# Prologue and first block of an attention and MoE kernel: ACT, VectorE and POOL in the order the code names them, with the weight conversion spread over the rounds

## The chip, the cores and the metric

The kernel runs on one core of one Trainium2 chip. The metric is the device time in microseconds (us) of one execution; 1224.36 us is the median of three runs of the kernel before. The engines are TensorE (PE in the rows; PEld is its weight load), VectorE (DVE), ScalarE (ACT), GpSimd (POOL) and SyncE (SP), which issues most of the DMAs.

## The reference

Chunked attention, then a dense gated layer, then a top-1 mixture of experts with a skip condition, over 4608 tokens of 512 features:

```python
scores = q_c @ k_c^T / sqrt(64)            # 8 batches, 8 heads, chunks of 64 of 576
attn   = softmax(scores);  x = attn @ v_c  # x: 4608 x 512
h = x @ w_in                               # 512 x 2048, w_in in float64
g = h * sigmoid(1.702 * h)
x = (g @ w_out)                            # 2048 x 512, w_out in float64
out = x
for tokens with x @ w_skip > 0:            # 8 experts, 512 x 1024 x 512
    e = argmax(x @ w_gate)
    out += softmax(x @ w_gate)[e] * relu(x @ w1[e]) @ w2[e]
```

All of it is to hold to float32. The kernel therefore splits each operand of a large product into a high part (`hi`, a type that TensorE takes at full rate) and a rest (`lo`), and adds three products: hi·hi, hi·lo, lo·hi.

## The kernel before

**Blocks and rounds.** The 4608 tokens are nine blocks of 512 (`j`), each of four tiles of 128. The dense layer runs block by block, and in a block over 16 rounds (`i`), one for each 128 of the 2048 hidden features. A round has `emit_h` (line 289: 12 matmuls h(i), with the weights `whi[i]`, `wlo[i]` and the activations `xh`, `xl`; then tanh on ScalarE and `sg` on VectorE), `emit_g` (line 303: `gh` on ScalarE, `gl` on VectorE) and `emit_y` (line 310: 12 matmuls y(i) into the four banks `ys`). h has two PSUM banks, so h(i+2) can start when sg(i) has been computed. After the nine blocks come the experts; they are not touched.

**Attention.** A tile's attention (`Att`, line 109) has `a` (transposes of q and k into qT, kT, copies on ScalarE), `b` (scores, maxima and differences on VectorE, exp on ScalarE), `c0` (sum, reciprocal and scaling on VectorE), `c1` (transposes pT, copy on ScalarE) and `d` (products with v, two copies into x1 on ScalarE). The four tiles of block 0 go through it in the prologue, in the seven turns of the loop over `tau` (line 710). The tiles of the next block go through it in the rounds of the block before: `burst` (line 214) has the scores of one tile and the v products of the tile before it, in the rounds 1, 4, 7, 10 and 13 of block 0 (`BURSTS`); `c0` and `c1` follow two rounds later, `a` stands one round ahead. Scores, v products, and the transposes of the rounds share two banks (`at`). At a block's end `split_x1` (line 280) makes `xh` and `xl` of the next block.

**The conversion of the weights.** w_in and w_out arrive as float64 in 32 halves of 128 x 512 (`Half`, line 232; half 2i is w_in of round i, half 2i+1 is w_out). No engine reads float64, so the bits are taken apart: `s0` makes `r` (from the high word) and `lf` (from the low word) on ScalarE; `s1` shifts `r` (line 262) and merges the sign (line 263) on VectorE and adds `lf` on POOL (line 264); `s3` makes `hi` on ScalarE (line 276) and `lo` on VectorE (line 277). Three buffers hold the raw halves; `load` issues one DMA of 512 KB on SP. `tick` (line 694) is one step m of this: s1 of half m, s0 of half m+1, s3 of half m-1, and the load of half m+3. `lf` has one buffer. 33 steps do all.

**What sets the order.** The program is recorded in the order of the code, and a planner then places the instructions of each engine by its own estimate of when their inputs are ready. Each engine executes its list in order and waits at each instruction for its inputs. The code calls `tick` once in each of the turns 1 to 6 and twice in each round of block 0, until the 33 steps are done.

Of the kernel before, what the change touches and what calls it, by code (L numbers as in the profile page):

```python
# [9 lines left out]
F32 = mybir.dt.float32  # L10
# [11 lines left out]
def kernel(  # L22
# [14 lines left out]
    PE, ACT, DVE, POOL, SP = nc.tensor, nc.scalar, nc.vector, nc.gpsimd, nc.sync  # L37
# [5 lines left out]
    P = 128  # L43
# [3 lines left out]
    NF = DFF // P  # L47
    BT = 512
    TPB = BT // P
# [11 lines left out]

    BURSTS = {0: (1, 4, 7, 10, 13)}
    BURSTN = (1, 5, 9, 13)
    NXT = NT // SL + NE + NSING + 2
    BIG = float(1 << 20)

# [4 lines left out]
    mp = ctx.enter_context(tc.tile_pool(name="main", bufs=1))  # L71
# [7 lines left out]
    def bank(shape, tag, name):  # L79
# [10 lines left out]
        fill=0.0, base=0, channel_multiplier=-1,  # L90
# [13 lines left out]
    emeta = cp.tile([1, 2, NE], U32, name="emeta")  # L104
    meta = cp.tile([1, 3, NXT], U32, name="meta")
    wgT = cp.tile([P, KD, NE + 1], F32, name="wgT")
# [123 lines left out]
    HW = KD * P  # L230

    class Half:
# [14 lines left out]
        def s0(self):  # L247
            bits = self.raw.bitcast(U32).rearrange("p (n two) -> p n two", two=2)
            self.hw = bits[:, :, 1]
            hwf = self.raw.bitcast(F32).rearrange("p (n two) -> p n two", two=2)[:, :, 1]  # L250
            self.r = mp.tile([P, HW], F32, tag="x2", name="r", bufs=4)
            self.lf = mp.tile([P, HW], F32, tag="junk", name="lf")


            ACT.activation(out=self.r, in_=hwf, func=AF.Abs, scale=2.0 ** -112)
            ACT.activation(out=self.lf.bitcast(U32), in_=bits[:, :, 0], func=AF.Copy, scale=2.0 ** -29)

        def s1(self):
# [3 lines left out]
            DVE.tensor_scalar(ru, ru, 3, None, op0=ALU.logical_shift_left)  # L262
            DVE.scalar_tensor_tensor(au, self.hw, 0x80000000, ru, op0=ALU.bitwise_and, op1=ALU.bitwise_or)
            POOL.tensor_tensor(au, au, self.lf.bitcast(U32), op=ALU.add)

        def s2(self):
            pass

        def s3(self):
            i, h = self.i, self.half  # L270
# [9 lines left out]
    def split_x1(x1):  # L280
        xh = mp.tile([P, KD, BT], F32R, tag="xh", name="xh")
        xl = mp.tile([P, KD, BT], F32R, tag="xl", name="xl")
        for kk in range(KD):
            src = x1[kk // 2][:, kk % 2]
            ACT.copy(out=xh[:, kk], in_=src)
            DVE.tensor_tensor(xl[:, kk], src, xh[:, kk].bitcast(F32), op=ALU.subtract)
        return xh, xl
# [12 lines left out]
        DVE.scalar_tensor_tensor(sg, sg, 1.0, ps, op0=ALU.add, op1=ALU.mult)  # L300
        return sg

    def emit_g(sg):
        gh = mp.tile([P, BT], F32R, tag="gh", name="gh", bufs=2)
        gl = mp.tile([P, BT], F32R, tag="gl", name="gl", bufs=2)
        ACT.activation(out=gh, in_=sg, func=AF.Copy, scale=0.5)  # L306
        DVE.scalar_tensor_tensor(gl, sg, 0.5, gh.bitcast(F32), op0=ALU.mult, op1=ALU.subtract)  # L307
        return gh, gl

# [127 lines left out]
    def extras():  # L437
# [7 lines left out]
        def wide(nm):  # L445
            t = m2.tile([P, DM], F32, tag="o", name=nm, bufs=2)
            return t[0:1, 0:NXT * NB2].rearrange("o (x b) -> o x b", b=NB2)

        xb = [1, NXT, NB2]
        rem, tu = m2s([1, NE], "rem"), m2s([1, NE], "tu", U32)  # L450
        bc, b0, b1 = m2s([1, 1, NB2], "bc"), m2s([1, 1, NB2], "b0"), m2s([1, 1, NB2], "b1")
        row0, dp = m2s([1, 1, NB2], "row0"), m2s([1, 1], "dp")
        ix, bj, cx = m2s([1, NXT, 1], "ix"), m2s([1, NXT, 1], "bj"), m2s([1, NXT, 1], "cx")

# [190 lines left out]
    fp = fstack.enter_context(tc.tile_pool(name="f64", bufs=1))  # L645
# [25 lines left out]
    x1 = new_x1()  # L671
    A = [Att(t, x1, t * P, ("y", "at", "h", "h"), pro_buf(t), ios[t]) for t in range(TPB)]
    halves = [Half(m) for m in range(2 * NF)]
# [18 lines left out]
    tick_n = [0]  # L692

    def tick():
        m = tick_n[0]
        tick_n[0] += 1
        if m == 0:
            halves[0].s0()
        if m < 2 * NF:
            halves[m].s1()  # L700
        if 1 <= m <= 2 * NF:
            halves[m - 1].s2()
        if m + 1 < 2 * NF:
            halves[m + 1].s0()
        if 1 <= m <= 2 * NF:
            halves[m - 1].s3()
        if m + 3 < 2 * NF:
            halves[m + 3].load()

    for tau in range(TPB + 3):  # L710
        if 0 <= tau - 2 < TPB:
            A[tau - 2].c0()
        if tau < TPB:
            A[tau].a()
        if 0 <= tau - 1 < TPB:
            A[tau - 1].b()
        if 0 <= tau - 2 < TPB:
            A[tau - 2].c1()
        if 0 <= tau - 3 < TPB:
            A[tau - 3].d()  # L720
        if tau >= 1:
            tick()
    for g in range(2):
        SP.dma_start(out=tv[g], in_=z)
    xh, xl = split_x1(x1)

    fill, late = [], []
    NST = NT // P - TPB
# [2 lines left out]
    for j in range(NB - 1):  # L731
        for i in BURSTS.get(j, BURSTN):
            round_of[j * NF + i] = len(round_of)
# [4 lines left out]
    for j in range(NB):  # L738
        lastb = j + 1 == NB
        if not lastb:  # L740
            x1 = new_x1()
        else:
            rs.close()
            rawp = rs.enter_context(tc.tile_pool(name="raw", bufs=2, side="right", reuse_waits="tile"))
            for _ in range(4):
                load_next()
        ys = [bank([P, DM], "y", "yps") for _ in range(TPB)]
        prev = None
        nf = len(fill)
        for i in range(NF):  # L750
            R = j * NF + i
            nc_ = round_of.get(R - 2)
            if nc_ is not None and nc_ < NST:
                St[nc_].c0()
            sg = emit_h(i, xh, xl)
            span = NF // 2 - 2 if lastb else NF - 5
            nfill = -(-len(fill) // (span - i)) if i < span else 0
            if nfill:
                fill.pop(0)()
                nfill -= 1  # L760
            if j == 0:
                tick()
                if i == 7:
                    gate_load()
                elif i == 11:
                    gate_rows()
            g = emit_g(sg)
            if prev is not None:
                emit_y(i - 1, prev, ys)
            na = round_of.get(R + 1)  # L770
            if na is not None and na < NST:
                St[na].a()
                if na + 1 < NST:
                    St[na + 1].load_qk()
            if nc_ is not None and nc_ < NST:
                St[nc_].c1()
            kb = round_of.get(R)
            if kb is not None:
                if kb:
                    St[kb - 1].x1 = x1  # L780
                burst(St[kb] if kb < NST else None, St[kb - 1] if kb else None)
                if kb < NST:
                    St[kb].load_v()
            if j == 0:
                tick()
            for _ in range(nfill):
                fill.pop(0)()
            if late and (i >= span or late[0][0] < j):
                late.pop(0)[1]()
            if lastb:  # L790
                if prev is not None:
                    conv_next2()
                if i == NF // 2:
                    gstack.close()
                    m2 = ctx.enter_context(tc.tile_pool(name="m2", bufs=1, reuse_waits="tile"))
                    for s in range(NEARLY):
                        slots[s].list(first_row(s))
                if i >= NF // 2 + 2 and i - NF // 2 - 2 < NEARLY:
                    slots[i - NF // 2 - 2].gather((NB - 1) * BT)
            prev = g  # L800
        if j == 0:
            while tick_n[0] <= 2 * NF:
                tick()
            fstack.close()
            gstack = ExitStack()
            gp = gstack.enter_context(tc.tile_pool(name="gates", bufs=1, reuse_waits="tile"))
            wg = gp.tile([P, NE, DM], F32, name="wg")
            ws = gp.tile([P, DM], F32, name="ws")
            SP.dma_start(out=ws, in_=w_skip.rearrange("(o d) -> o d", o=1).to_broadcast([P, DM]))
            SP.dma_start(  # L810
                out=wg, in_=wgd[0:NE].rearrange("(o e) d -> o e d", o=1).to_broadcast([P, NE, DM]))
        if not lastb:
            xhn = split_x1(x1)
            emit_y(NF - 1, prev, ys)
            xh, xl = xhn
        else:
            slots[0].trans()
            emit_y(NF - 1, prev, ys)
            conv_next2()
        xs = evac_y(j, ys)  # L820
        lg = new_lg()
        if not lastb:
            fill = [lambda t=t, e=e, lg=lg, xs=xs: dot(lg, xs, t, e) for t in range(TPB) for e in range(NE + 1)]
            rt = route(j, lg)
            if j == NB - 3:
                rt.insert(3, order)
            late += [(j + 1, f) for f in rt]


    jx = m2.tile([1, NXT, 1], F32, name="jx")  # L830
    jw = m2.tile([1, NXT, 1], F32, name="jw")
    jm = m2.tile([1, NXT, 1], F32, name="jm")
# [103 lines left out]
```

## Time and profile before

| | us |
|---|---|
| median of three runs (1224.11, 1226.07, 1224.36) | 1224.36 |
| the profiled execution's own time | 1227.84 |
| its span, first to last instruction | 1226.1 |
| TensorE busy in the span | 1182.7 (96%) |
| VectorE busy | 783.9 (64%) |
| ScalarE busy | 490.2 (40%) |
| POOL busy | 144.6 (12%) |

How to read it: a busy time is the sum of an engine's instructions, an average over stages. A timeline row gives start, duration, engine, line, operation and tiles of one or several like instructions, and in brackets the idle time of the engine just before and what ended it. Matmuls overlap in the pipeline, so their rows are longer than their distance from one to the next.

### The profile page before, as it was taken

The numbers are of one execution on the slowest core, as the hardware profiler recorded it, in microseconds if no ns is written. First come the engines' busy times: TensorE is split into PE (matmuls) and PEld (weight loads), VectorE is DVE, ScalarE is ACT, GpSimd is POOL, SyncE is SP. The second block draws the span as 40 slices with busy tenths as digits, with TensorE's granted clock in tenths as the row PEclk, the third lists the DMA queues.
The fourth block names the chain that finished last, engine by engine and source line by source line (L and its number), as shares of the span: only waits on it lengthen the run. The fifth ranks groups of instructions, "written<-read, shape, count | busy, mean of one in ns | idle before, by whom it ended". The sixth has DMA issues, their size and how long they took to land. (4 is left out here: it accounts for less than half of the span.)

```text
span 1226.1 us, 20893 instructions
## 1 busy us (share of the span) xinstructions
PE 1182.7 (96%) x7984; PEld 991.8 (81%) x7984; DVE 783.9 (64%) x1771; ACT 490.2 (40%) x825; POOL 144.6 (12%) x137
## 2 busy tenths in 40 slices
PE   6798999999999999999999999999999999999995
PEld 4576788888888888888888888888788989999885
DVE  5889578369349548647736935943985686665531
ACT  5867443343332333324334333332344454444320
POOL 2344000010010010000001001001021023231110
PEclk9999999999999999999999999999999999999998
DMA  9756331131122113113113113202344677666540
GB/s 211 208 175 178 112 102 27 44 104 26 27 68 78 28 31 107 32 31 95 35 36 104 26 28 92 55 10 69 130 139 131 215 170 265 215 228 227 195 144 8
DMA packets 181848, 129.00 MB, mean 105 GB/s; under 512 B 122336, under 2 KB 155360, under 8 KB 181617
## 3 DMA queue, kind: packets, MB, share of 16 engines
q1 hardware_dynamic: 177072, 117.09, 33.4%
q0 software_dynamic: 4672, 10.54, 2.5%
q8 instruction: 64, 1.05, 0.4%
q14 instruction: 40, 0.32, 0.1%
HBM read 103.59 MB, written 25.04 MB: 105 GB/s over the span
## 5 line engine op out<-in xcount | busy, mean ns | idle before, releaser
L316 PE MATMUL yps<-whi,gh 128*128 128x512 f32 x576 | 228.7, 397 | 6.4 <-ACT gh L306 6.4
L296 PE MATMUL hps<-xh,whi 128*128 128x512 f32 x576 | 231.6, 405 | 3.2 <-DVE sg L300 3.2
L296 PE MATMUL hps<-xl,whi 128*128 128x512 f32 x576 | 227.5, 395 | 0.0
L296 PE MATMUL hps<-xh,wlo 128*128 128x512 f32 x576 | 227.0, 394 | 0.0
L317 PE MATMUL yps<-wlo,gh 128*128 128x512 f32 x576 | 225.6, 392 | 0.0
L300 DVE SCALAR_TENSOR_TENSOR sg<-sg,hps 128x512 f32<-128x512 f32 x144 | 98.3, 684 | 172.1 <-ACT sg L299 171.1
L353 DVE CUSTOM_DVE_ANT_0 junk<-x,wg 128x512 f32<-128x512 f32 x256 | 175.8, 687 | 4.0
L543 DVE TENSOR_TENSOR elo<-rawe,ehi 128x1024 fp32r<-128x1024 f32 x88 | 107.6, 1224 | 84.6 <-ACT ehi L542 84.5
L320 PE MATMUL yps<-whi,gl 128*128 128x512 f32 x576 | 156.0, 393 | 0.0
L299 ACT ACTIVATE sg<-hps 128x512 f32<-128x512 f32 x144 | 85.8, 598 | 163.4 <-PE hps L296 163.2
L542 ACT CAST ehi<-rawe 128x1024 fp32r<-128x1024 f32 x88 | 92.3, 1049 | 139.6 <-PE h2p L608 69.4
L306 ACT ACTIVATE gh<-sg 128x512 fp32r<-128x512 f32 x144 | 91.0, 632 | 118.3 <-DVE sg L300 104.8
L316 PEld LDWEIGHTS yps<-whi,gh 128*128 128x128 f32 x576 | 108.3, 188 | 30.9 <-ACT gh L306 7.8
L296 PEld LDWEIGHTS hps<-xh,whi 128*128 128x128 f32 x576 | 108.5, 190 | 26.3 <-DVE sg L300 4.1
L296 PEld LDWEIGHTS hps<-xh,wlo 128*128 128x128 f32 x576 | 108.9, 189 | 22.6
L320 PEld LDWEIGHTS yps<-whi,gl 128*128 128x128 f32 x576 | 108.0, 189 | 22.6 <-DVE gl L307 0.3
L317 PEld LDWEIGHTS yps<-wlo,gh 128*128 128x128 f32 x576 | 108.5, 188 | 21.8
L296 PEld LDWEIGHTS hps<-xl,whi 128*128 128x128 f32 x576 | 109.2, 190 | 20.6
L307 DVE SCALAR_TENSOR_TENSOR gl<-sg,gh 128x512 fp32r<-128x512 f32 x144 | 99.0, 688 | 33.4 <-ACT gh L306 21.7
L406 POOL DMA_INDIRECT tab<-pr,pos x36 | 37.8, 1049 | 682.3 <-DVE st L166 335.0
L608 PE MATMUL h2p<-xT,ehi 128*128 128x256 f32 x640 | 117.2, 283 | 0.0
L608 PEld LDWEIGHTS h2p<-xT,ehi 128*128 128x128 f32 x640 | 101.9, 191 | 2.6
(172 smaller groups left out, 1520.5 us busy)
## 6 DMA issues: line engine op xcount, KB each, us to landing
rawe<-in_moe_w_dram SPq DMA_DIRECT2D x88, 512.0 KB, 4.0
v<-in_v_dram SPq DMA_DIRECT2D x144, 64.0 KB, 2.7
x2d<-x SPq DMA_DIRECT2D x36, 256.0 KB, 3.1
out_dram<-x SPq DMA_DIRECT2D x36, 256.0 KB, 3.8
q<-in_q_dram SPq DMA_DIRECT2D x32, 256.0 KB, 3.7
k<-in_k_dram SPq DMA_DIRECT2D x32, 256.0 KB, 3.7
raw<-in_moe_w_in_dram SPq DMA_DIRECT2D x16, 512.0 KB, 4.0
raw<-in_moe_w_out_dram SPq DMA_DIRECT2D x16, 512.0 KB, 3.3
```

The source lines that it names most:

```text
L296: PE.matmul(ps, a, b[:, kk], start=(n == 0), stop=(n == 3 * KD - 1))
L299: ACT.activation(out=sg, in_=ps, func=AF.Tanh, scale=0.851)
L300: DVE.scalar_tensor_tensor(sg, sg, 1.0, ps, op0=ALU.add, op1=ALU.mult)
L306: ACT.activation(out=gh, in_=sg, func=AF.Copy, scale=0.5)
L307: DVE.scalar_tensor_tensor(gl, sg, 0.5, gh.bitcast(F32), op0=ALU.mult, op1=ALU.subtract)
L316: PE.matmul(ys[t], gh[:, cs], wh, start=first, stop=False)
L317: PE.matmul(ys[t], gh[:, cs], wl, start=False, stop=False)
L320: PE.matmul(ys[t], gl[:, cs], wh, start=False, stop=last)
L353: DVE.tensor_tensor_reduce(junk, xs[t], wg[:, e, :] if e < NE else ws, 1.0, 0.0, ALU.mult, ALU.add, lg[:, t, e:e + 1])
L542: ACT.copy(out=hi, in_=raw)
L543: DVE.tensor_tensor(lo, raw, hi.bitcast(F32), op=ALU.subtract)
L608: PE.matmul(ps[:, f], a[:, c], self.xT[:, b, kk], start=(m == 0), stop=(m == 3 * KD - 1))
```

## The change

It hands the planner three engines' lists as they are written: from the loop over `tau` to the end of block 0, `tc.manual_schedule` makes ScalarE, VectorE and POOL take their instructions in the order of the code. TensorE and SP are still placed by the planner. The code's order is changed with it: two steps more in the turns 5 and 6 make eight by the end of the prologue (`NTICK0`); the other 25 are spread evenly up to round 14 (`ticks_by`: 10 steps done after round 0, then 12, 13, 15, 17, 18, ... 33), in each round the first of them in two halves: `tick1` (s1) between gh and gl, `tick2` (s3, s0, load) behind gl; a second one stands before the burst. `split_x1` of block 0 moves ahead of the last two steps of the prologue. In a step s3 now stands ahead of s0. `lf` gets a second buffer. The empty `s2` goes.

```diff
+    NTICK0 = 8
...
-            self.lf = mp.tile([P, HW], F32, tag="junk", name="lf")
+            pool, tag = ((mp, "junk"), (fp, "lf"))[self.half]
+            self.lf = pool.tile([P, HW], F32, tag=tag, name="lf")
...
-    def emit_g(sg):
+    def emit_g(sg, between=None):
...
         ACT.activation(out=gh, in_=sg, func=AF.Copy, scale=0.5)
+        if between is not None:
+            between()
         DVE.scalar_tensor_tensor(gl, sg, 0.5, gh.bitcast(F32), op0=ALU.mult, op1=ALU.subtract)
...
+    def tick1():
         m = tick_n[0]
-        tick_n[0] += 1
         if m == 0:
             halves[0].s0()
         if m < 2 * NF:
             halves[m].s1()
+
+    def tick2():
+        m = tick_n[0]
+        tick_n[0] += 1
         if 1 <= m <= 2 * NF:
-            halves[m - 1].s2()
+            halves[m - 1].s3()
         if m + 1 < 2 * NF:
             halves[m + 1].s0()
-        if 1 <= m <= 2 * NF:
-            halves[m - 1].s3()
         if m + 3 < 2 * NF:
             halves[m + 3].load()
 
+    def ticks_by(i):
+
+        return min(2 * NF + 1, NTICK0 - (-(2 * NF + 1 - NTICK0) * (i + 1) // (NF - 1)))
+
+    inorder = ExitStack()
+    inorder.enter_context(tc.manual_schedule(engines={ACT.engine, DVE.engine, POOL.engine}))
     for tau in range(TPB + 3):
...
+        if tau == TPB + 2:
+            xh, xl = split_x1(x1)
         if tau >= 1:
+            tick()
+        if tau > TPB:
             tick()
...
+            mid = None
             if j == 0:
-                tick()
...
+                if tick_n[0] < ticks_by(i):
+                    mid = tick1
+            g = emit_g(sg, mid)
+            if mid is not None:
+                tick2()
...
+            while j == 0 and tick_n[0] < ticks_by(i):
+                tick()
...
-            if j == 0:
-                tick()
...
         if j == 0:
-            while tick_n[0] <= 2 * NF:
-                tick()
+            inorder.close()
```

Three places of the lists show what moves. A number behind a name is the tile's; the changed file has its lines up to 23 later.

ScalarE at the end of the prologue, before: `r`, `lf` and `hi` are the conversion, line 212 is a copy into x1, line 285 is xh.

```order
L189 COPY bA_97<-pTp_418 128x512
L255 ACTIVATE r_480<-raw64_412 128x512
L212 COPY x1_99<-pv0_424 128x2x128
L256 ACTIVATE lf_481<-raw64_412 128x512
L276 CAST whi_484<-a_476 128x512
L255 ACTIVATE r_534<-raw64_454 128x512
L256 ACTIVATE lf_535<-raw64_454 128x512
L276 CAST whi_572<-a_530 128x512
L212 COPY x1_100<-pv1_425 128x2x128
L212 COPY x1_99<-pv0_456 128x2x128
```

And now (lines 191, 214 and 258 are the former 189, 212 and 255):

```order
L191 COPY bA_97<-pTp_420 128x512
L214 COPY x1_99<-pv0_426 128x2x128
L214 COPY x1_100<-pv1_427 128x2x128
L276 CAST whi_406<-a_402 128x512
L258 ACTIVATE r_452<-raw64_346 128x512
L259 ACTIVATE lf_453<-raw64_346 128x512
L276 CAST whi_462<-a_446 128x512
L258 ACTIVATE r_466<-raw64_414 128x512
L259 ACTIVATE lf_467<-raw64_414 128x512
L214 COPY x1_99<-pv0_472 128x2x128
L214 COPY x1_100<-pv1_473 128x2x128
L285 CAST xh_492<-x1_99 128x512 x2
```

The copies of tile 2 follow the pT copy of tile 3 directly; between them and those of tile 3 stand six conversion instructions of two steps, and behind these xh.

ScalarE around the second burst of block 0, before (line 173 is exp, 299 is tanh, 306 is gh):

```order
L212 COPY x1_508<-sv0_853 128x2x128
L299 ACTIVATE sg_927<-hps_914 128x512
L173 ACTIVATE qT_776<-qT_776 128x512
L212 COPY x1_509<-sv1_854 128x2x128
L255 ACTIVATE r_1184<-raw64_1084 128x512
```

And now, from the pT copy of round 3 to the tanh of round 5 (line 175 is exp):

```order
L191 COPY qT_579<-pTp_805 128x512
L276 CAST whi_765<-a_760 128x512
L258 ACTIVATE r_817<-raw64_723 128x512
L259 ACTIVATE lf_818<-raw64_723 128x512
L299 ACTIVATE sg_836<-hps_823 128x512
L306 ACTIVATE gh_839<-sg_836 128x512
...
L175 ACTIVATE qT_792<-qT_792 128x512
L214 COPY x1_536<-sv0_881 128x2x128
L214 COPY x1_537<-sv1_882 128x2x128
L299 ACTIVATE sg_941<-hps_928 128x512
```

The tanh of a round stands behind the pT copy and the conversion of the round before, and behind exp and both copies of a burst; before, the tanh stood ahead of exp.

TensorE at the same burst, before: the last matmuls of y(3), then the rest of the v products (line 207) and the scores (158), then h(5).

```order
L320 MATMUL yps_513<-whi_572,gl_756 128x512
L207 MATMUL sv1_854<-qT_551,v_646 64x64
...
L158 MATMUL sv1_854<-kT_783,qT_776 64x64
L296 MATMUL hps_914<-xh_492,whi_717 128x512
```

And now the last matmul of h(5), those of y(3), then pT, v products and scores, then h(6):

```order
L296 MATMUL hps_928<-xh_492,wlo_655 128x512
L318 MATMUL yps_538<-whi_518,gh_757 128x512
...
L322 MATMUL yps_541<-whi_518,gl_758 128x512
L189 MATMUL pTp_805<-ident_72,qT_579 128x128 x4
L209 MATMUL sv0_881<-qT_579,v_688 64x64
...
L160 MATMUL sv1_882<-kT_799,qT_792 64x64
L296 MATMUL hps_978<-xh_492,whi_765 128x512
```

TensorE is now one round further ahead at this burst, and the pT transposes, which stood ahead of h(2), stand behind h(5) and y(3).

## Rows read from the trace of the kernel before

**Rows 1.** Busy time by stage: length, each engine's busy us, granted clock, DMA share, GB/s.
```profile
0.00:48.70 48.70, 29.92 (x352) 23.71 (x353) 30.96 (x66) 29.59 (x56) 13.21 (x22) 1.00 0.94 219
48.70:124.00 75.30, 66.97 (x395) 51.87 (x394) 69.77 (x108) 55.58 (x101) 34.51 (x22) 0.98 0.60 175
80.00:90.00 10.00, 10.00 (x73) 7.75 (x72) 9.56 (x15) 6.80 (x12) 5.69 (x4) 0.83 0.63 185
124.00:157.00 33.00, 33.00 (x273) 26.87 (x272) 18.41 (x34) 15.07 (x30) 2.63 (x2) 1.00 0.33 105
```

**Rows 2.** Timeline of TensorE, prologue to the start of block 1.
```profile
11.93 1.12 PE L141 MATMUL kTp<-ident,k 128*128 128x128 f32 x4
...
48.73 1.20 PE L296 MATMUL hps<-xh,whi 128*128 128x512 f32 x2
...
58.27 0.50 PE L296 MATMUL hps<-xh,whi 128*128 128x512 f32 x1 [1.41 <-DVE sg L300]
...
69.89 0.39 PE L316 MATMUL yps<-whi,gh 128*128 128x512 f32 x1
...
72.61 0.39 PE L296 MATMUL hps<-xh,whi 128*128 128x512 f32 x1
...
78.88 0.50 PE L316 MATMUL yps<-whi,gh 128*128 128x512 f32 x1 [2.99 <-ACT gh L306]
...
144.93 0.60 PE L187 MATMUL pTp<-ident,qT 128*128 128x128 f32 x4
...
159.55 0.71 PE L296 MATMUL hps<-xh,whi 128*128 128x512 f32 x2
```

**Rows 3.** Timeline of VectorE in the prologue.
```profile
26.49 0.69 DVE L176 TENSOR_REDUCE st<-bA 128x8 f32<-128x512 f32 x1 [0.32 <-ACT bA L173]
...
27.66 0.69 DVE L179 TENSOR_TENSOR bA<-bA,st 128x512 f32<-128x512 f32 x1
...
30.79 0.43 DVE L262 TENSOR_SCALAR r<-r 128x512 uint32<-128x512 uint32 x1 [1.37 <-ACT r L255]
...
31.86 0.75 DVE L166 TENSOR_REDUCE st<-s 128x4 f32<-128x256 f32 x2
32.52 0.74 DVE L168 TENSOR_TENSOR bA<-s,st 128x256 f32<-128x256 f32 x2
```

**Rows 4.** Timeline of ScalarE at the end of the prologue.
```profile
41.67 0.67 ACT L255 ACTIVATE r<-raw 128x512 f32<-128x512 f32 x1 [1.04 <-DMA raw<-in_moe_w_out_dram]
...
47.00 0.36 ACT L212 COPY x<-pv 128x256 f32<-128x256 f32 x1
```

**Rows 5.** Single lines up to 160 us: count, duration in ns (least, median, most), first and last start.
```profile
L277 DVE TENSOR_TENSOR wlo<-a,whi x32: 653/904/1782, 18.1 to 145.9; 128x512 fp32r<-128x512 f32 x32
...
L264 POOL TENSOR_TENSOR a<-a,lf x32: 1262/1341/4091, 14.4 to 143.6; 128x512 uint32<-128x512 uint32 x32
...
L263 DVE SCALAR_TENSOR_TENSOR a<-raw,r x32: 674/684/1659, 13.6 to 141.7; 128x512 uint32<-128x512 uint32 x32
...
L307 DVE SCALAR_TENSOR_TENSOR gl<-sg,gh x16: 674/683/693, 59.7 to 159.9; 128x512 fp32r<-128x512 f32 x16
...
L300 DVE SCALAR_TENSOR_TENSOR sg<-sg,hps x16: 672/678/687, 57.5 to 156.9; 128x512 f32<-128x512 f32 x16
...
L255 ACT ACTIVATE r<-raw x32: 648/672/695, 12.4 to 140.0; 128x512 f32<-128x512 f32 x32
```

**Rows 6.** Timelines of POOL and VectorE: two of the POOL adds and their neighbours.
```profile
59.56 4.09 POOL L264 TENSOR_TENSOR a<-a,lf 128x512 uint32<-128x512 uint32 x1 [0.81 <-ACT lf L256]
...
101.52 1.85 POOL L264 TENSOR_TENSOR a<-a,lf 128x512 uint32<-128x512 uint32 x1 [0.78 <-ACT lf L256]
...
101.54 0.68 DVE L307 SCALAR_TENSOR_TENSOR gl<-sg,gh 128x512 fp32r<-128x512 f32 x1
102.14 1.78 DVE L277 TENSOR_TENSOR wlo<-a,whi 128x512 fp32r<-128x512 f32 x1
```

**Rows 7.** DMA issues: queue, operation, count, KB each, median us from issue to landing.
```profile
raw<-in_moe_w_in_dram SPq DMA_DIRECT2D x16, 512.0 KB, 4.0
```

More of the change, by code (lines that the diff above doesn't have):

```diff
@@ L264, in s1 @@
             POOL.tensor_tensor(au, au, self.lf.bitcast(U32), op=ALU.add)
-        def s2(self):
-            pass
         def s3(self):
@@ L694, in tick @@
     def tick():
+        tick1()
+        tick2()
+    def tick1():
         m = tick_n[0]
-        tick_n[0] += 1
         if m == 0:
@@ L724 @@
         SP.dma_start(out=tv[g], in_=z)
-    xh, xl = split_x1(x1)
     fill, late = [], []
@@ L748 @@
         prev = None
-        nf = len(fill)
+        if j == 0:
+            assert tick_n[0] == NTICK0
         for i in range(NF):
@@ L766 @@
                     gate_rows()
-            g = emit_g(sg)
+                if tick_n[0] < ticks_by(i):
+                    mid = tick1
+            g = emit_g(sg, mid)
+            if mid is not None:
+                tick2()
             if prev is not None:
@@ L801 @@
         if j == 0:
-            while tick_n[0] <= 2 * NF:
-                tick()
+            inorder.close()
+            assert tick_n[0] == 2 * NF + 1
             fstack.close()
```

## Prediction

> **What bounds the kernel now.** I read the busy times by stage first. From 124 us on TensorE is busy in 33.0 of 33.0 us [rows 1], and the two programs give TensorE the same order from the middle of block 1 to the end. So whatever the first 160 us gain or lose arrives unchanged at the end, and I measure everything at one mark: the first h product of block 1 (round 16), which starts at 159.55 us [rows 2].
>
> Before that mark there are two stages. The prologue lasts until h(0) at 48.73 [rows 2], with TensorE busy 29.9 of 48.7 us [rows 1]: a chain over ScalarE, VectorE and TensorE. Then block 0, where until 124 us VectorE is busy 69.8 of 75.3 us and TensorE 67.0 [rows 1]: 8.3 us of TensorE are lost to waits such as the 2.99 us for gh [rows 2], while the conversion of the weights takes VectorE.
>
> Third view, the order of the instructions beside the timeline. In the prologue VectorE waits 1.37 us for a conversion's r at 30.79, and the scores' maxima of tile 3, which wait for nothing later than that, come after it at 31.86 [rows 3]. On ScalarE the last x1 copy stands behind a wait of 1.04 us for a weight load and several conversions; it runs at 47.00 [rows 4], and the split of x1 and h(0) follow.
>
> Fourth, the durations [rows 5], and what the POOL add does to VectorE. An add takes 1.26 us when undisturbed. The subtraction lo takes 0.65 at the least, 1.78 at the most; gl always 0.67 to 0.69. The pair at 101.5 shows why: the add, asked for at 101.52, runs when gl ends at 102.2, and lo, which began at 102.14, ends only at 103.92, 0.55 after the add [rows 6].
>
> **Part 1, the prologue in the named order.** A turn on VectorE is now lo, the softmax's sum and scaling (c0), scores (b), one conversion step. lo is 0.65; c0 is 1.86 (26.49 to 28.35); b is 1.40 (31.86 to 33.26) [rows 3]; the step's shift and merge are 0.46 + 0.69 [rows 3, 5]. With about 0.6 of waiting for hi that is 5.8 us a turn. The first c0 starts at 15.9: tile 1's second transposes end at 13.05 [rows 2], and then come, one behind the other, copy 0.59, exp 0.53, r 0.67 and the step's 1.15. The next follow at 22.3 (0.6 more, for the first hi), 28.1 and 33.8. Tile 3's c0 is done at 35.4, its transposes and copy at 37.1. Then ScalarE does, in its new order, two x1 copies, hi, r, lf, hi, r, lf (six of 0.5 to 0.6 each and two of 0.3, to 41.0), the last x1 copies (41.4), xh. So h(0) starts at **42.0**, 6.7 us earlier than now. Cover: r of half 6 must have landed by 39.7; a weight load takes 4.0 us [rows 7], and the step that frees its buffer is done at 32. Without that cover the term shrinks by the lateness, so I keep 4 to 8 us.
>
> **Part 2, rounds 0 to 2.** From h(0) to h(2), the wait for sg(0) included, it takes 9.5 us now, with a tile's transposes (48.73 to 58.27 [rows 2]), and some 8.5 without, so sg(0) ends at 50.4. Round 0 has two steps; from gh(0) to tanh(1) ScalarE has ten instructions of 0.5 to 0.6, and sg(0) stands ahead: 6.2 us from sg(0) to sg(1). Round 1 has two steps and a burst, 8.9 us (below). sg(2) starts at **64.9**. Now TensorE is at h(4) at 72.61 [rows 2] with one y more done; there it would be at 65.6. With that y (2.72 us, 69.89 to 72.61 [rows 2]) only 4.3 of the 6.7 us are left.
>
> **Part 3, the rounds in the named order.** The two h banks let TensorE run two rounds ahead at most: h(i+2) needs sg(i). So the distance from one sg to the next sets the pace. Rounds come in threes, with 1, 2 and 2 steps. Successive independent instructions start about 0.08 before the last ends, which the terms include.
> - One step, then c0: sg 0.60, shift 0.46, merge 0.61, gl 0.68, POOL add 1.26, rest of lo 0.55, c0 1.86 [rows 3, 5, 6]: **5.9**.
> - Two steps with the pT copy. sg(3) lets h(5) start. TensorE's list then has y(3), and only then the transposes pT; ScalarE's list has the pT copy ahead of hi, r, lf and tanh(4). sg 0.68, h 2.72, y 2.72, pT 0.60 [rows 2], copy 0.59, hi, r, lf 1.65, tanh 0.6: **9.6**.
> - Two steps with the burst: sg 0.60, shift and merge 1.07, gl 0.68, add 1.26, lo 0.55, shift and merge 1.07, lo 0.60, b 1.40, exp 0.63, two x1 copies 0.5, and only then tanh 0.6: **8.9**.
>
> Together 24.4 us for three rounds. TensorE itself has six products of 2.72 and about 3 us of attention there, 19.3. So 5 us are lost every three rounds, and they go on to round 14, because the steps are spread to the last round. Now the steps come faster and are nearly over at 121: from 124 on nothing is lost.
>
> sg(2) 64.9, sg(5) 89.3, sg(8) 113.7. From round 9 TensorE's list has y(9) before the pT products, so gh stands in the chain too: sg(9) 119.6, sg(10) 129.9 (10.3), sg(11) 138.8, sg(12) 144.8, sg(13) 152.3 (7.5), sg(14) 161.2. Then sg, gh and y(14), 4.1: round 16 starts at 165.3. That is 5.7 us later than 159.55. Two groups of transposes (0.60 each [rows 2]) that stand ahead of the mark now come behind it, and h of round 16 has to wait for each part of xl: I put 1.8 for both. **Sum: 7.5 us later.**
>
> **The other edits.** The second lf buffer frees r and lf of the next half from the POOL add; it costs nothing and is in the walk. Each step issues one 512 KB load on SP. Some stand behind a tile's v loads, which wait for the last tile's products; a load is needed two steps after its buffer is free, some 9 us at 4.9 us a step (24.4 over 5), against 4.0 to land [rows 7]. Removing s2 removes nothing.
>
> **The unknown price** is the add against lo: nine of these rounds have a lo behind an add. Below, zero: at 59.56 an add took 4.09, so four VectorE instructions went first [rows 6]. Above, 1.26 each. I take 1.26, because the nearest row, with gl ahead and lo behind, shows it. A gain from the add has no mechanism.
>
> The profiled execution is 1227.84 us (span 1226.1), 3.5 above the median 1224.36. 1227.84 + 7.5 - 3.5 = **1232 us**.
>
> **Rivals.** A measurement of this kernel can tell some 0.2%, 2.4 us, from no change.
> 1. *VectorE goes first.* If lo starts right behind gl and the add waits, nine times 1.26 = 11 us leave the chain: round 16 at 156, **1221 us**, faster. It decides at five of the nine. For it: the row at 59.56. Against: that is one add; the others look like 101.52. The Trainium skill (SBUF — State Buffer, SBUF: two separate sides) calls the shared pair an exclusive lock that goes to whichever instruction starts first; by that rule lo, next in VectorE's queue, could hold it and 1221 comes out. The row at 101.52 gives it to the add, which had asked before. Chance 0.14.
> 2. *TensorE paces.* If the distances above overlap better than I walked them, block 0 loses nothing: from 42.0, the 110.8 us between the marks less 8.3 of idle and 1.5 of lowered clock (0.98 over 75.3 us) [rows 1], so 143, **1208 us**. For it: VectorE's own work in three rounds, 15.4 us without waiting (sg and gl three times 1.28, five steps of 1.67, c0 1.86, b 1.40), is under TensorE's 19.3. Against: the places of tanh behind exp and pT are fixed, and an engine that waits in order cannot go round them. The Trainium skill (Perfetto Trace Analysis, Identifying the Most-Contended Engine) names the engine with the highest occupancy as the one to judge by, which here would be TensorE and this case. Chance 0.08.
> 3. *It cancels.* A prologue 2 us better and three of the adds not in the way: **1224 us**. Chance 0.13.
> 4. *The clock drops too.* Every three rounds TensorE would idle 2 us and more ahead of a tile's transposes; behind the 2.99 us at 78.88 the granted clock of the stretch from 80 to 90 is 0.83 [rows 1, 2], that is, part of it at 1.2 GHz: 17% of 10 us, 1.7. If that comes in each of the five threes, five times 1.7 are 8.5 more: **1241 us**. Chance 0.10.
>
> TensorE and SP are still ordered by the planner, so "in the order named" holds for three engines only; that is in the walk and no case of its own.
>
> **Numbers.** The forecast has 0.55. Its own range is 1227 to 1238. Eight in ten reach from 1217 (leaving out rival 2 and the far end of 1) to 1241. Faster 0.22 (rivals 1 and 2), same 0.13, slower 0.65.
>
> **What would show it.** h(0) between 41 and 45. Three rounds at 24 us, 22 if lo goes first, 19.4 if TensorE paces. In the list of waits: hps waiting for sg, qTp for the x1 copies and ScalarE's copy for pTp should grow. VectorE should be less busy than now from 60 to 120, and still converting at 150. I am wrong if three rounds take under 22 us or if round 16 starts before 157.

## The result, and the profile after

The changed kernel takes 1243.6 us (median of four runs, 1240.25 to 1244.04) against 1225.21 us (1224.11 to 1226.31) for the kernel before on the same chip: ratio 1.0141, 95% interval [1.0128, 1.0154], so 18.4 us slower. Forecast were 1232 and a range up to 1241: the direction was right, the size too small. The profiled execution took 1244.04 us of its own, span 1242.3, which is 16.2 more than the span before, where 7.5 were forecast.

Busy time by stage, as in [rows 1], with one stage more up to the mark:
```profile
0.00:48.44 48.44, 27.64 (x312) 21.21 (x312) 23.41 (x52) 23.93 (x46) 9.64 (x19) 1.00 0.87 189
48.44:124.00 75.56, 67.78 (x423) 52.96 (x424) 60.26 (x94) 47.75 (x88) 26.28 (x17) 0.95 0.51 149
124.00:157.00 33.00, 28.43 (x231) 22.38 (x232) 25.18 (x41) 19.64 (x37) 10.58 (x7) 0.95 0.43 129
157.00:173.00 16.00, 13.56 (x75) 10.36 (x67) 12.83 (x24) 9.51 (x19) 3.29 (x3) 0.89 0.28 91
```
TensorE, full from 124 us before, now idles 4.6 of 33 us there, and VectorE, less busy up to 124 than before (60.3 for 69.8), is still converting after 157. Both were in the forecast. The prologue was not: it was to end at 42.0 and ends at 48.47, hardly earlier than before (48.73).

**The prologue.** TensorE, ScalarE and VectorE, their timelines put together in order of time:
```profile
31.46 1.09 PE L189 MATMUL pTp<-ident,bA 128*128 128x128 f32 x4 [3.14 <-DVE bA L181]
...
32.48 1.12 PE L209 MATMUL pv<-bA,v 64*64 64x64 f32 x16
...
33.52 1.11 PE L143 MATMUL qTp<-ident,q 128*128 128x128 f32 x4
...
35.09 1.08 PE L143 MATMUL kTp<-ident,k 128*128 128x128 f32 x4 [0.46 <-DMA k<-in_k_dram]
...
36.11 1.12 PE L209 MATMUL pv<-bA,v 64*64 64x64 f32 x16
...
37.27 0.37 ACT L214 COPY x<-pv 128x256 f32<-128x256 f32 x1 [3.15 <-PE pv L209]
37.54 0.62 ACT L276 CAST whi<-a 128x512 fp32r<-128x512 f32 x1
...
38.20 0.69 DVE L277 TENSOR_TENSOR wlo<-a,whi 128x512 fp32r<-128x512 f32 x1 [4.50 <-ACT whi L276]
...
38.81 0.68 DVE L178 TENSOR_REDUCE st<-bA 128x8 f32<-128x512 f32 x1
...
40.80 1.09 PE L189 MATMUL pTp<-ident,bA 128*128 128x128 f32 x4 [3.57 <-DVE bA L181]
...
48.47 1.22 PE L296 MATMUL hps<-xh,whi 128*128 128x512 f32 x2 [3.20 <-ACT xh L285]
```
This is one turn, and it closes on itself: transposes pT (31.46), v products in two groups with the transposes qT and kT of the next block's first tile between them (33.52 to 36.11), x1 copies (37.27), hi (37.54), lo (38.20), the next c0 (38.81), the next pT (40.80). In the named order hi stands behind the x1 copies, and VectorE's lo, with c0 behind it, waits 4.50 us.

**The rounds.** VectorE, POOL and ScalarE over one group of three rounds, put together in order of time:
```profile
86.67 0.69 DVE L300 SCALAR_TENSOR_TENSOR sg<-sg,hps 128x512 f32<-128x512 f32 x1 [0.95 <-ACT sg L299]
...
88.59 1.57 POOL L267 TENSOR_TENSOR a<-a,lf 128x512 uint32<-128x512 uint32 x1 [5.06 <-ACT whi L276]
...
88.94 1.78 DVE L277 TENSOR_TENSOR wlo<-a,whi 128x512 fp32r<-128x512 f32 x1
...
92.29 0.75 DVE L168 TENSOR_REDUCE st<-sv 128x4 f32<-128x256 f32 x2
...
94.85 0.61 ACT L299 ACTIVATE sg<-hps 128x512 f32<-128x512 f32 x1
...
95.49 0.69 DVE L300 SCALAR_TENSOR_TENSOR sg<-sg,hps 128x512 f32<-128x512 f32 x1 [1.79 <-ACT sg L299]
...
97.41 1.58 POOL L267 TENSOR_TENSOR a<-a,lf 128x512 uint32<-128x512 uint32 x1 [3.89 <-ACT whi L276]
...
97.76 1.78 DVE L277 TENSOR_TENSOR wlo<-a,whi 128x512 fp32r<-128x512 f32 x1
...
101.23 0.68 DVE L300 SCALAR_TENSOR_TENSOR sg<-sg,hps 128x512 f32<-128x512 f32 x1
...
108.22 0.58 ACT L191 COPY qT<-pTp 128x512 f32<-128x512 f32 x1 [2.99 <-PE pTp L189]
...
110.38 0.59 ACT L299 ACTIVATE sg<-hps 128x512 f32<-128x512 f32 x1
...
111.00 0.69 DVE L300 SCALAR_TENSOR_TENSOR sg<-sg,hps 128x512 f32<-128x512 f32 x1 [0.95 <-ACT sg L299]
```
From sg to sg: 8.82 with the burst, 5.74 with one step, 9.77 with the pT copy, together 24.33 where 24.4 was forecast (8.9, 5.9, 9.6). The two lo's of 1.78 end 0.56 and 0.55 after an add on POOL, as in [rows 6] (0.55). The chain of the pT round runs as walked: ScalarE waits 2.99 for pT, and hi, r, lf and tanh stand behind the copy.

The list of waits from 48 to 173 us (us in total, times, longest):
```profile
ACT qT L191 <- PE pTp L189: 10.6, 4, 3.7
ACT gh L306 <- PE yps L322: 9.1, 3, 3.0
PE hps L296 <- DVE sg L300: 6.1, 6, 1.6
```
Of the three that were to grow, two are there (before, from 48 to 160, hps waited once for sg, 1.4 us, and the copy for pTp is not in the list); the third, qTp for the x1 copies, hardly grew (0.9 us, as the weight load's wait, for 0.8 before).

**The last round of the block**, TensorE:
```profile
168.54 0.50 PE L318 MATMUL yps<-whi,gh 128*128 128x512 f32 x1 [1.92 <-ACT gh L306]
...
169.62 0.63 PE L318 MATMUL yps<-whi,gh 128*128 128x512 f32 x1
170.04 0.63 PE L319 MATMUL yps<-wlo,gh 128*128 128x512 f32 x1
...
171.32 1.83 PE L322 MATMUL yps<-whi,gl 128*128 128x512 f32 x4
172.99 0.39 PE L296 MATMUL hps<-xh,whi 128*128 128x512 f32 x1
```
The last row is the mark, the first h of round 16: 13.4 us later than the 159.55 of [rows 2]. y(14) takes 4.45 us instead of 2.72: it comes after 1.92 us of waiting, and from 169.62 on its products stand 0.42 to 0.43 apart instead of 0.23. The granted clock from 170 to 172 is 0.50, the lower of TensorE's two levels.

### The profile page after: what moved, and what is told of

The parts are those of the page before. It is cut to its first block, busy times and chain, and to the rows that moved or that the text cites. A ratio compares the mean times of both kernels' runs of the same rounds, so it can differ in the third digit from the quotient of the medians.

```text
span 1242.3 us, 20863 instructions
## 1 busy us (share of the span) xinstructions
PE 1189.5 (96%) x7984; PEld 995.7 (80%) x7984; DVE 784.9 (63%) x1771; ACT 488.5 (39%) x825; POOL 146.2 (12%) x137
```

## The experiments

The changed kernel is the base of all but f1. Ratios are to the kernel before on the same chip, with 95% intervals. That kernel's median was 1225.2 to 1227.8 us on the chips used, so small differences between runs are read from the ratios. The changed kernel's ratio is 1.0141.

**1. Order or spread?** Three kernels take the named order away in parts.
```diff
 e1: closed before block 0
+    inorder.close()
     for j in range(NB):
 e2: opened before block 0 instead of before the prologue
 e3: never opened
```


> The named order holds for the prologue only; block 0 goes back to the planner, with the new spread of the steps. Theory (the loss is made in the rounds, by ScalarE and VectorE standing behind their fixed lists: 24.3 us for three rounds): h(0) stays at 48.5, three rounds take about 20.5, round 16 starts between 156 and 162, 1220 to 1227 us. Rival (the loss comes from the spread itself, conversions that run on to 165 and hold a round up wherever the order is from): round 16 at 172 or later, 1237 us or more.

> The planner orders the prologue (with eight steps in it), the named order begins with block 0. Theory: the rounds lose the same 17 us; the prologue in the planner's order, two steps longer than before, reaches h(0) at 49 to 52: 1241 to 1246 us. Rival (the prologue's fixed order is what loses, the rounds would recover if started at the planner's state): 1226 to 1232 us.

> No named order at all; eight steps in the prologue, the rest spread, s3 ahead of s0 and the second lf buffer stay. Theory (order, not spread): 1221 to 1228 us, round 16 near 159. Rival (spread, not order): 1237 us or more, with VectorE's lo late in rounds 13 to 15.

Measured: e1 1231.33 us, 1.0035 [1.0022, 1.0048]; e2 1241.47, 1.0122 [1.0102, 1.0143]; e3 1228.18, 1.0017 [1.0007, 1.0027]. So it is the order: with the same spread and no named order 0.17% is left (0.07 to 0.27), little beside 1.41. Most of it is the order of the rounds: e2, with block 0 alone in the named order, still loses 1.22%, and e1, with the prologue alone, 0.35%. I missed two things. In e1 the planner, left to itself behind a named prologue, brought attention of block 0's rounds ahead of h(0), which came at 52.63, and conversions ahead of sg(0). TensorE then waited as below, round 16 started at 164.54, and e1 lies 4 us above my range (and 6 under the rival's):
```profile
67.36 0.80 PE L296 MATMUL hps<-xh,whi 128*128 128x512 f32 x1 [6.44 <-DVE sg L300]
```
In e2 the prologue got shorter, not longer. TensorE:
```profile
44.54 1.22 PE L296 MATMUL hps<-xh,whi 128*128 128x512 f32 x2 [0.99 <-ACT xh L285]
```
With eight steps in it, and ScalarE's, VectorE's and POOL's work of block 0 out of its hands, the planner's prologue reaches h(0) 4.2 us earlier than before and 3.9 earlier than the named one; in e3, where it may move that work, h(0) is at 49.05. The rounds behind it keep their distances to 0.1 us (sg(4) to sg(7) 24.30).

**2. The second lf buffer alone**, in the kernel before.
```diff
-            self.lf = mp.tile([P, HW], F32, tag="junk", name="lf")
+            pool, tag = ((mp, "junk"), (fp, "lf"))[self.half]
+            self.lf = pool.tile([P, HW], F32, tag=tag, name="lf")
```


> The kernel before with the second lf buffer alone. Theory (it frees nothing that was waited for): within 0.2% of the kernel before. Rival (lf of the next half no longer waits for the POOL add, and the conversions come earlier): 3 to 5 us faster.

Measured: 1225.77 us, 0.9999 [0.9989, 1.0009]. That edit costs and brings nothing.

**3. Where the prologue's gain went.** First, TensorE in the order of the code too:
```diff
-tc.manual_schedule(engines={ACT.engine, DVE.engine, POOL.engine})
+tc.manual_schedule(engines={ACT.engine, DVE.engine, POOL.engine, PE.engine})
```
(in the prologue alone).

> TensorE takes the prologue's instructions in the order of the code too, so that the v products of tile 0 and the scores stand as I walked them. Theory (h(0) missed 42.0 because ScalarE's x1 copies waited for v products that the planner had put late in TensorE's list, 3.15 us at 37.27, and hi, lo and the last c0 stood behind them): that wait falls to under 1.5, h(0) at 45 to 47, 1240 to 1243 us. Rival (the x1 copies cost nothing, ScalarE is bound by its own work): h(0) stays at 48.5 and the time at 1243.5.

Measured: 1247.25 us, 1.0166 [1.0144, 1.0187], h(0) at 50.30: a miss. In the code a tile's transposes stand ahead of the scores of the tile before, so the first scores waited for the second tile's q (12.86 instead of 7.17 us), and the next block's qT and kT still stood within the v products (35.48 to 37.38). The last turn did fall from 9.34 to 8.28 us, but that was less than the start cost. Then the place of the step:
```diff
+        if tau >= 1:
+            tick()
         if 0 <= tau - 3 < TPB:
             A[tau - 3].d()
         if tau == TPB + 2:
             xh, xl = split_x1(x1)
-        if tau >= 1:
-            tick()
         if tau > TPB:
             tick()
```


> In a turn of the prologue the conversion step stands ahead of the v products' x1 copies instead of behind them; nothing else. Theory (a loop that my walk did not have: c0, transposes pT, v products, x1 copies, hi, lo, next c0; in it the next block's qT and kT, 2.6 us): lo's wait of 4.50 us at 38.20 falls to under 2, the last c0 goes from 38.81 to 34 to 36, h(0) from 48.47 to about 45.3 (TensorE is then held by tile 4's transposes until 37), 1240 to 1241 us. Rival (ScalarE's own work bounds the prologue): h(0) stays within 1 us of 48.5.

Measured: 1243.03 us, 1.0123 [1.0106, 1.014]. VectorE, ScalarE and TensorE:
```profile
33.72 1.28 DVE L277 TENSOR_TENSOR wlo<-a,whi 128x512 fp32r<-128x512 f32 x1 [0.71 <-ACT whi L276]
...
34.92 0.67 DVE L178 TENSOR_REDUCE st<-bA 128x8 f32<-128x512 f32 x1
...
44.56 0.66 ACT L258 ACTIVATE r<-raw 128x512 f32<-128x512 f32 x1 [1.53 <-DMA raw<-in_moe_w_out_dram]
...
46.87 1.22 PE L296 MATMUL hps<-xh,whi 128*128 128x512 f32 x2 [4.67 <-ACT xh L285]
```
lo waits 0.71 instead of 4.50, and the four c0's start at 15.85, 22.63, 28.78 and 34.92, near my walk's 15.9, 22.3, 28.1 and 33.8. So the loop was what the walk of these turns lacked. Little of it reaches h(0), 46.87 where I expected 45.3: this edit puts a third step ahead of xh, and its r waits 1.53 for its weights. Then the split first:
```diff
+        if 1 <= tau <= TPB + 1:
+            tick()
         if 0 <= tau - 3 < TPB:
             A[tau - 3].d()
         if tau == TPB + 2:
             xh, xl = split_x1(x1)
-        if tau >= 1:
             tick()
-        if tau > TPB:
+            tick()
             tick()
```
(five steps ahead of the v products, three behind the split).

> The same, and of the eight steps the last three stand behind the last x1 copies and the split of x1. Theory (six of ScalarE's 0.5 to 0.6 us instructions leave the path to xh): h(0) at 42 to 43, and everything behind it as much earlier, since the rounds keep their distances: 1236 to 1238 us. Rival (what is gained at h(0) is paid back in round 0, where ScalarE has the three steps ahead of tanh): sg(0) stays at 55 or later, 1240 us or more.

Measured: 1243.16 us, 1.0122 [1.0096, 1.0149]. h(0) came at 43.90, 0.9 over its 42 to 43, but sg(0) at 54.23 is only 2.5 earlier than in the changed kernel (56.77): in the steps behind the split hi waited 2.13 and 1.00 us for POOL's adds, ahead of tanh(0). ScalarE:
```profile
49.21 0.62 ACT L276 CAST whi<-a 128x512 fp32r<-128x512 f32 x1 [2.13 <-POOL a L267]
...
51.98 0.62 ACT L276 CAST whi<-a 128x512 fp32r<-128x512 f32 x1 [1.00 <-POOL a L267]
```
The time is the rival's; sg(0) lies between the two.

**4. The add against lo**, the unknown price. Two kernels: hi and lo ahead of shift, merge and add, and no add at all.
```diff
 r1: in a step
+            halves[m - 1].s3()
             halves[m].s1()
-            halves[m - 1].s3()
     and in a round the whole first step behind gl
-                if tick_n[0] < ticks_by(i):
-                    mid = tick1
+                mid = None
             g = emit_g(sg, mid)
-            if mid is not None:
-                tick2()
+            if j == 0 and tick_n[0] < ticks_by(i):
+                tick()
 n1: in s1
-            POOL.tensor_tensor(au, au, self.lf.bitcast(U32), op=ALU.add)
```


> In a step hi and lo of the half before stand ahead of shift, merge and POOL add, so that no lo stands behind an add. Theory (an add that has asked first keeps VectorE's next operation with two inputs from SBUF waiting, and 1.1 us of it stand in two of three rounds): lo back to 0.65 to 0.7, three rounds from 24.3 to about 22, 1233 to 1236 us. Rival (the lock only moves to the next such operation, the merge): three rounds stay at 24 and merge takes up to 1.8, 1242 to 1245 us.

> The changed kernel without the POOL add: the low words of the weights are converted but not added in, so that hi and lo lack them; all else is the same. Theory (the add's hold on lo is on the path in two of three rounds): lo 0.65 to 0.7 throughout, the round with one step 5.7 to 4.6 or TensorE's 5.4, the burst's round 8.8 to 7.7, the pT round stays at 9.7: three rounds 22 to 22.8 us, 1234 to 1238 us. Rival (the hold lies beside other waits and the price was 0): three rounds stay at 24 and over, 1242 to 1245 us.

r1 measured 1268.95 us, 1.0332 [1.0314, 1.0349]: far off both. lo did fall to 0.69 everywhere and the merge stayed at 0.69, but (VectorE, POOL, ScalarE)
```profile
102.21 0.69 DVE L266 SCALAR_TENSOR_TENSOR a<-raw,r 128x512 uint32<-128x512 uint32 x1
103.07 1.29 POOL L267 TENSOR_TENSOR a<-a,lf 128x512 uint32<-128x512 uint32 x1 [2.62 <-DVE a L266]
104.39 0.62 ACT L276 CAST whi<-a 128x512 fp32r<-128x512 f32 x1 [2.14 <-POOL a L267]
...
105.05 0.69 DVE L277 TENSOR_TENSOR wlo<-a,whi 128x512 fp32r<-128x512 f32 x1 [2.14 <-ACT whi L276]
...
106.11 0.69 DVE L266 SCALAR_TENSOR_TENSOR a<-raw,r 128x512 uint32<-128x512 uint32 x1
```
merge, add, hi, lo and the next merge now wait for one another, 3.9 us a step. In the change hi and lo of one half stand behind the merge of the next, so that an add has most of a step's time to finish. r1 also moved shift, merge and add from ahead of gl to behind it, so its loss of 25 us is not the price of the new order alone. n1 measured 1235.37 us, 1.0079 [1.006, 1.0098], VectorE:
```profile
69.44 0.69 DVE L299 SCALAR_TENSOR_TENSOR sg<-sg,hps 128x512 f32<-128x512 f32 x1 [1.24 <-ACT sg L298]
...
74.08 0.68 DVE L299 SCALAR_TENSOR_TENSOR sg<-sg,hps 128x512 f32<-128x512 f32 x1
...
84.61 0.69 DVE L299 SCALAR_TENSOR_TENSOR sg<-sg,hps 128x512 f32<-128x512 f32 x1 [0.95 <-ACT sg L298]
...
92.35 0.69 DVE L299 SCALAR_TENSOR_TENSOR sg<-sg,hps 128x512 f32<-128x512 f32 x1 [1.79 <-ACT sg L298]
```
One step 4.64, the burst 7.74, the pT round 10.53 instead of the 9.7 that should have stayed: 22.91 for 24.3. The hold is on the path, 1.1 in each of two rounds, and the third round takes 0.8 back. The ratio falls from 1.0141 to 1.0079, some 7.6 us.

**5. The places in the rounds.** First the pT copy a round later, then also tanh and sg ahead of the burst:
```diff
 r2
+            late_c1 = j == 0 and R < NF - 1
-            if nc_ is not None and nc_ < NST:
+            if nc_ is not None and nc_ < NST and not late_c1:
                 St[nc_].c1()
+            if late_c1 and round_of.get(R - 3) is not None:
+                St[round_of[R - 3]].c1()
 r3, besides
-            sg = emit_h(i, xh, xl)
+            sg = ahead.pop(0) if ahead else emit_h(i, xh, xl)
...
+            if j == 0 and kb is not None:
+                ahead.append(emit_h(i + 1, xh, xl))
```


> In block 0 the transposes pT and their copy move from the round behind c0 to the next one, behind its first step, so that tanh of that round no longer stands behind TensorE's h, y, pT. Theory (fixed places: in that round 9.8 us go from sg to sg, of which h 2.72, y 2.72 and pT 0.6 are waited for): that round falls to 7 to 7.5, but the burst's products now stand behind h and y, and the burst's round grows from 8.8 to about 10.4: three rounds 23 us, 1237 to 1239 us. Rival (the burst's round does not grow): three rounds 21.5 us, 1231 us; or TensorE's list hides it all: 24.3.

> On top of the later pT copy, tanh and sg of the round behind a burst stand ahead of the burst's exp, x1 copies and maxima. Theory (the rounds' length is the sum along the fixed lists, so what is taken out of the list ahead of tanh comes off the time): the burst's round falls from 10.9 to about 7, three rounds to 21 to 21.5 us, now near VectorE's own 20.9 (15.4 of work and five times 1.1 behind an add), 1229 to 1233 us, 1.002 to 1.006 of the kernel before. Rival (gh now stands behind exp and the x1 copies, and y waits for it): three rounds stay at 23, 1238 us.

r2: 1238.03 us, 1.0083 [1.0066, 1.01]; the pT round takes 6.19 (7 to 7.5 forecast), the burst's 10.87 (10.4), three rounds 22.8 and 23.2, about the 23 forecast. r3: 1230.29 us, 1.0038 [1.0025, 1.0051]. VectorE in r3:
```profile
87.76 0.69 DVE L300 SCALAR_TENSOR_TENSOR sg<-sg,hps 128x512 f32<-128x512 f32 x1
...
108.27 0.69 DVE L300 SCALAR_TENSOR_TENSOR sg<-sg,hps 128x512 f32<-128x512 f32 x1
```
Three rounds 20.51; the others are 19.4 to 21.5, somewhat under the 21 to 21.5 forecast. The parts were missed: the burst's round fell to 5.83 instead of 7, and the round behind it, not in my walk, rose from 5.74 to 8.58. No work was added or taken away; tanh, sg and the pT copy stand elsewhere on ScalarE's and VectorE's lists, and the products that go with them may move on TensorE's. 13 of the 18 us came back.

**6. Both repairs, and two tries at more.** c2 is e6 and r3 together; c3 and b1 are
```diff
 c3: c2, and
-                elif i == 11:
+                elif i == 12:
                     gate_rows()
 b1: opened before block 0, as in e2, and
             prev = g
+            if R == 0:
+                inorder.close()
```

> The prologue with the step ahead of the v products and the split ahead of the last three steps, and the rounds with the later pT copy and the earlier tanh. Theory (the two losses add up): h(0) at 44, three rounds at 21 to 21.5, 1227 to 1230 us, no faster than the kernel before, since TensorE's 19.3 is still not reached. Rival (once the rounds are near TensorE's pace the earlier start is hidden by it): same as with the rounds alone.

> The two repairs together, and the gate rows' transposes and copies one round later (round 12 instead of 11), where the banks are free. Theory (a single wait): the 2.51 us ahead of the gate rows' transposes goes, the mark comes 2 to 3 us earlier, 1224 to 1226 us, level with the kernel before within 0.2%. Rival (VectorE's load paces the rounds, and the wait only hides in it): 1227 to 1228 us as without.

> The planner orders the prologue and rounds 1 to 15; only round 0 is in the named order (spread steps, eight in the prologue). Theory (the planner's prologue reaches h(0) at 44.5 when nothing of the rounds is put into it, and its rounds take the 110.8 us from h(0) to the first h of block 1 that they took before): 1221 to 1225 us, at or under the kernel before. Rival (the planner's rounds run worse from there, as with the named prologue where sg(0) came at 64): 1229 to 1232 us.

c2: 1227.31 us, 1.0013 [1.0003, 1.0022], h(0) at 42.70: 0.13% over the kernel before and in the forecast range. The two gains add up, 3 us beyond r3. In c2's trace round 16 starts at 155.49, 4.1 us ahead of [rows 2], and the first h of block 2 is 2.1 us ahead. The time is not lower even so: the profiled execution of the kernel before took 3.5 us more than its median, and a lead of 2 us over one execution decides nothing. c3: 1226.82 us, 1.0013 [1.0002, 1.0024]. TensorE:
```profile
131.79 0.60 PE L342 MATMUL wgp<-ident,wgT 128*8 128x128 f32 x4 [2.51 <-ACT x L214]
```
The wait is still there: the planner put the transposes behind the same burst again. So the theory was not tested, and what that wait costs stays open. b1: 1231.93 us, 1.0056 [1.0039, 1.0073]. h(0) was at 44.54 as expected, and the planner's rounds lost it again (the rival). No version here beats the kernel before.

## Why the prediction was right about the direction and short by 11.6 us

**What held.** That the rounds are paced by the fixed lists and not by TensorE: three rounds 24.3 for 24.4, sg(0) to sg(1) 6.13 for 6.2, sg(8) to sg(14) 47.3 for 47.5. r2 and r3 changed the length by moving a few instructions, and the sums came out about as the same walk forecast, in r3 with two misses in the parts that cancel. That the price of the add against lo is near its upper bound: n1 shows 1.1 for each lo on the path (1.26 assumed), though without any add the whole gain was 7.6 us and not nine times that. That the second lf buffer costs nothing: f1. And that a loss before the mark goes through to the later blocks: the first h of block 2 starts 15.4 us later than before, and the lag is the same 15.4 at the first h of block 8. Before, then after:
```profile
258.86 0.71 PE L296 MATMUL hps<-xh,whi 128*128 128x512 f32 x2
274.30 0.71 PE L296 MATMUL hps<-xh,whi 128*128 128x512 f32 x2
```

**The step that failed is part 1**, "With about 0.6 of waiting for hi that is 5.8 us a turn". The turns took 6.78, 7.12 and 9.34. I walked VectorE's turn with hi ready 0.6 later, and did not follow what stands ahead of hi on ScalarE's list: the x1 copies, which wait for v products, which TensorE, still ordered by the planner, takes behind pT, behind c0; and in the last turn the next block's qT and kT stand among them too. I had read TensorE's list and called its planner "in the walk". With the step ahead of the copies, e5's turns are 6.78, 6.15 and 6.14. The loop made the last c0 5.0 us late (38.81 for 33.8). From there to h(0) it took 9.7 for the 8.2 walked; there two more x1 copies wait 0.47 and 0.38 for v products, and the rest stays open. So h(0) came 6.5 us late, and 5.9 are left at sg(14) (167.14 for 161.2), after small misses of both signs (round 1 took 8.3 for 8.9).

**Three more terms were mis-sized.** y(14) at the lower clock: 1.7, so the mark came at 172.99 for 165.3. Behind the mark the lag grew by 2.8 for 1.8: by 2.0 up to the first h of block 2, near the forecast, and by 0.8 behind the first h of block 8 (13.8 at the last h, 16.2 at the end). The change does not touch that part, and one execution of each kernel does not show where the 0.8 comes from. These and the 5.9 are the 8.7 by which the span missed, but for rounding. The rest, 3.1, is the step to the median: I took 3.5 off because the profiled execution before lay that far above its median; that of the changed kernel lies 0.4 above. (8.7 and 3.1 are 11.8; the forecast had been rounded up by 0.2.)

Some sums of the prediction do not come out as printed: the terms of a turn add up to 5.7 for the 5.8, those of the round with one step to 6.0 for 5.9, those of the burst's round to 9.0 for 8.9, and 11 us less would put rival 1's round 16 at 154, not 156. None of it moves the forecast by 1 us.

**Rivals.** *VectorE goes first* is refuted, by lo's 1.78 and by n1. *TensorE paces* is refuted too, by three rounds of 24.3 for its 19.3. The page behind it, the Trainium skill (Perfetto Trace Analysis, Identifying the Most-Contended Engine), calls the engine with the highest occupancy the most contended and has it optimized first. Over the span that is TensorE, busy 96%, and r3 and c2 changed the time by 1 to 1.3% with its work unchanged. In block 0 up to 124 us it is VectorE in the kernel before, 69.8 us to 67.0 [rows 1], and TensorE in the changed one, 67.8 to 60.3. Neither share shows the waits that made the loss. *It cancels* is refuted by 1243.6. *The clock drops too* came true in the rows (0.95 for 0.98 from 48 to 124, 0.89 up to the mark) but hardly in the sum: the groups of three rounds with a slow stretch took 24.3, 24.3 and 25.0 for the 24.4, 24.4 and 25.1 walked at the upper clock. In the first of them h(6), from 87.41 on, ran at the lower clock, and the next h still had to wait for sg:
```profile
96.23 0.50 PE L296 MATMUL hps<-xh,whi 128*128 128x512 f32 x1 [0.40 <-DVE sg L300]
```
The lower clock counted only in the last round.

## What to carry to other kernels

When an engine is told to keep an order, look for a loop: follow each instruction that it waits for back through the other engines' lists until you are at the first engine again, one turn later; the loop's length is the turn, whatever the engines' own work adds up to. A planner's order that looks untidy may be what hides these waits, and a named order has to place the few instructions that others wait for (here tanh, hi and the copy of pT) ahead of those that nobody waits for. Naming three of four engines leaves the loops through the fourth as the planner made them; naming the fourth as well was no cure by itself (e4).

## What the runs showed of the hardware

An add on POOL that asked while VectorE was busy went next in the rows read here, ahead of VectorE's next instruction: lo 1.78 behind it, 0.69 without any add (n1). The one exception is the add at 59.56 in [rows 6], which took 4.09; no other add in these traces took over 1.85. Why four VectorE instructions went ahead of that one stays open. I had expected the hold for operations with two inputs from SBUF. In e1 an operation with one input was held as well, a shift that takes 0.42 otherwise; VectorE:
```profile
56.23 1.52 DVE L265 TENSOR_SCALAR r<-r 128x512 uint32<-128x512 uint32 x1
```
The Trainium skill (SBUF — State Buffer, SBUF: two separate sides) puts VectorE operations in a two-port mode and those with two SBUF inputs under one lock with GpSimd. For lo the rows agree; of the shift they show that it was held, not in which mode it ran.

In these traces every instruction that reads a raw half reads it as f32 or uint32 words, and products with operands of hi's type stand 0.23 us apart at the upper clock (96.57 to 96.80 in the changed kernel). No run tests whether an engine could read float64, or another type in hi's place.

Whether the time lost to the lower clock could be had back by keeping TensorE busy in its waits was not tried.
